# Sliding the moving operands of a two-layer MLP by 16 bytes per revolution of their ring

## The chip, the cores and the metric

The kernel runs on one core of one Trainium2 chip. The metric is device time in microseconds (us) of one execution; lower is better. The engines that matter are TensorE (PE in the rows; its weight loads have a row kind of their own, PEld), VectorE (DVE), ScalarE (ACT), GpSimd (POOL) and SyncE (SP), which here only issues DMAs.

## The reference, cut to what matters

```python
X = np.fft.rfft(x, axis=1)                       # x: 8 x 3008 x 256
y = np.fft.irfft(X * (filt_r + 1j * filt_i)[None], n=3008, axis=1)
x = y.reshape(24064, 256)
h = x @ w_in                                     # 256 -> 2048
P = a[0] + a[1] * h + a[2] * h**2 + a[3] * h**3
Q = 1 + abs(b[0]) * abs(h) + abs(b[1]) * h**2
out = (P / (Q + 1e-6)) @ w_out                   # 2048 -> 256
```

A long convolution by Fourier transforms along the sequence, then an MLP with a rational activation on 24064 tokens.

## The kernel before

The tokens are cut into 47 tiles of 512 (`T`), and the 2048 hidden features into 16 blocks of 128. One tile with one block is a *unit*: 752 units, the last of them split into two halves of 256 tokens, so 753. Both products of the MLP are done with a split of each float32 number into an upper and a lower part of type fp32r: upper times upper, upper times lower, lower times upper. One unit therefore has six matmuls for the first product (`product_in`, lines 631, 632 and 634: two of each, over the two halves of the 256 input features) and six for the second (`product_out`, lines 714, 715 and 716: two of each, over the two halves of the 256 outputs). In all twelve the weights are the stationary operand (128 x 128) and the tokens are the moving one (128 partitions x 512 columns of 4 bytes).

Where the moving operands lie:

- The split inputs are in one tile `xhl`, [128, 4, 1536] (`RX` = 1536 columns = three token tiles), whose first two rows are `xh` (upper parts of the two feature halves) and whose last two are `xl`. It is a ring: token s lies in column s % 1536. The ring goes round 15 times and two thirds in the 47 tiles. The convolution fills it chunk by chunk in `stage3`: float32 matmuls into PSUM (line 590), ScalarE writes the upper part (line 604), VectorE subtracts and writes the lower (line 606). Most chunks are 470 tokens long, and a chunk can start at any multiple of 47 tokens; a chunk that crosses the end of the ring is written in two parts.
- The results of the activation are in the tiles `hi` (five buffers) and `lo` (four), 128 x 512 of fp32r each. VectorE writes `hi` (`g_hi`, line 691) and `lo` (`g_lo`, line 705), GpSimd reads `hi` once (`pool_m`, line 696).

In the built program every tile named here starts at a multiple of 256 bytes within its partition, the weights `wi_sb` and `wo_sb` included (each 128 x 128 block of them is 512 bytes wide). So all twelve moving operands of every unit start at a multiple of 256 bytes, and so do their stationary operands. Two operands elsewhere do not: `e_sb`, the moving operand of line 590, starts 960 bytes into `small_sb`, so 192 bytes past a multiple of 256, and every second matmul of that line starts 188 bytes further, 124 bytes past one, which is not a multiple of 16 bytes. And the chunks that lines 604 and 606 write into the ring start at any multiple of 188 bytes.

The order of the instructions on PE, ACT, DVE and POOL is that in which the code issues them (a `manual_schedule`); a unit's second product is issued four units (`LAG`) after its first. Convolution steps are put between the units by a credit counter until the last batch is done. All DMAs are issued by SyncE.

Of the kernel before, what the change touches and what calls it, by code (L numbers as in the profile page):

```python
# [10 lines left out]
F32R = mybir.dt.float32r  # L11
# [26 lines left out]
RING = dict(a=4, w=3, q=5, hi=5, lo=4)  # L38
# [22 lines left out]
T = 512  # L61
RX = 1536
TT = 512


def shape_constants():
# [116 lines left out]
def conv_moe(ctx: ExitStack, tc: tile.TileContext, xp, filt, w_in, w_out, mats, small, sgn, outT):  # L183
    nc = tc.nc
    B = xp.shape[0]

    consts = ctx.enter_context(tc.tile_pool(name="consts", bufs=1))
    dram = ctx.enter_context(tc.tile_pool(name="dram", bufs=3, space=DRAM))
    conv = ctx.enter_context(tc.tile_pool(name="conv", bufs=2))
    mlp = ctx.enter_context(tc.tile_pool(name="mlp", bufs=1))  # L190
# [3 lines left out]
    sgn_sb = consts.tile([128, 32], F32, name="sgn_sb")  # L194
    wi_sb = consts.tile([128, 4, 2, 2, TT], F32R, name="wi_sb")
    wo_sb = consts.tile([128, 8, 2, TT], F32R, name="wo_sb")
    tin0 = consts.tile([128, K2, C], F32, tag="xhl", name="tin0")
# [53 lines left out]
    class Weights:  # L251
# [12 lines left out]
        def load(self):  # L264
# [5 lines left out]
            else:  # L270
                raw = conv.tile([128, TT, 2], U32, tag=tag, name=f"raw{i}", **({"bufs": bufs} if bufs else {}))
            self.l, self.h = raw[:, :, 0], raw[:, :, 1]
            nc.sync.dma_start(raw.rearrange("p c t -> p (c t)"), self.src)

        def room(self):
            i = self.i
            if i in FIRST:
                self.p, self.t = (
                    mlp.tile([128, TT], U32, tag=slots[2 * (FIRST.index(i) % 8) + n], name=f"{x}{i}")
                    for n, x in enumerate(("wp", "wt"))  # L280
                )
            else:
                pt = conv.tile([128, 2, TT], U32, tag="f2", name=f"wp{i}", bufs=FB)
                self.p, self.t = pt[:, 0], pt[:, 1]
# [54 lines left out]
    def w_in_part(k, f, cc):  # L339
        return wi_sb[:, f // 4, cc, k, f % 4 * 128 : f % 4 * 128 + 128]  # L340
# [19 lines left out]
    class Banks:  # L360
# [5 lines left out]
        def tile(self, name):  # L366
            k = min(self.free, key=self.free.get)
            del self.free[k]
            return k, ps.tile([128, TT], F32, tag=f"h{k}", name=name)

# [200 lines left out]
    def stage3(k):  # L571

        b, r, n = chunks[k]
        tiles, five = n * 2 // 5 if n % 5 == 0 else n // 2, n % 5 == 0
        tl = conv.tile([128, 4, C], F32, tag="tl", name=f"tl{k}")
        scr = scr2[b].rearrange("k (e r) c -> (k e) r c", e=2)
        for h in range(2):
            nc.sync.dma_start(tl[h * RH : h * RH + RH, :tiles], scr[:, r + h * tiles : r + h * tiles + tiles])
        if five:
            src = scr[:, r + 2 * tiles : r + n].rearrange("(k e) s c -> k e (s c)", e=2)  # L580
            nc.sync.dma_start(tl[2 * RH : 2 * RH + K2].rearrange("p (e s) c -> p e (s c)", e=2), src)
        if five:
            steps = [(2 * RH + K2, 2 * e + s, 5 * s + 2 * e, 1 - e, 4 - e) for s in range(2) for e in range(2)]
        else:
            steps = [(2 * RH, u, 2 * u, 1, 3) for u in range(tiles)]
        for cc in range(2):
            yield 1.1
            bank, pt = banks.tile(f"x_{k}_{cc}")
            for m, (rows, u, o, e0, e1) in enumerate(steps):
                nc.tensor.matmul(  # L590
                    pt[:, o * N2 : (o + e1 - e0) * N2],
                    tl[:rows, u, cc * 128 : cc * 128 + 128],
                    e_sb[:rows, e0 * N2 : e1 * N2],
                    start=m == 0,
                    stop=m == len(steps) - 1,
                    skip_group_check=True,
                )
            yield

            t0, t1 = spans[k]  # L600
            cut = min(t1, (t0 // RX + 1) * RX)
            parts = [(slice(a % RX, a % RX + z - a), pt[:, a - t0 : z - t0]) for a, z in ((t0, cut), (cut, t1)) if a < z]
            for o, p in parts:
                nc.scalar.activation(xh[:, cc, o], p, AF.Copy)
            for o, p in parts:
                v.tensor_tensor(out=xl[:, cc, o], in0=p, in1=xh[:, cc, o].bitcast(F32), op=ALU.subtract)
            banks.done(bank, 0.5)

    xh = xl = None
    pos = {}  # L610

    class Unit:

# [4 lines left out]
            self.p0 = P0 if squares else A0  # L618

        def tile(self, tag, dt=F32):  # L620
            full = mlp.tile([128, TT], dt, tag=f"{tag}{self.i % RING[tag]}", name=f"{tag}_u{self.i}")
            return full[:, self.cols]

        def product_in(self):
            self.bank, o = banks.tile(f"h_u{self.i}")
            o = self.H = o[:, self.cols]
            first = self.t * T % RX
            ts = slice(first + self.cols.start, first + self.cols.stop)
            f = self.f
            for cc in range(2):  # L630
                nc.tensor.matmul(o, w_in_part(0, f, cc), xh[:, cc, ts], start=cc == 0, stop=False)  # L631
                nc.tensor.matmul(o, w_in_part(0, f, cc), xl[:, cc, ts], start=False, stop=False)  # L632
            for cc in range(2):
                nc.tensor.matmul(o, w_in_part(1, f, cc), xh[:, cc, ts], start=False, stop=cc == 1)  # L634
# [103 lines left out]
    whole, parts = slice(0, T), [slice(c, c + T // LAST) for c in range(0, T, T // LAST)]  # L738
# [14 lines left out]
    def head():  # L753

        plan = Plan(8 - T * 2 // TT, dict(xin=XB, oe=2, tl=2, ev=2, f1=FB, f2=FB, raw=1))
        s = Stage2(0)
        first, sums, pts, yts, zts, pair = {}, {}, {}, {}, {}, []

        def x_load(t):
            n, tag = width(t), ("xin", "xin", "xin", "xin", "oe", "oe", "tl")[t]  # L760
            if tag == "tl":
                tile = conv.tile([128, 4, C], F32, tag=tag, name=f"xin0_{t}")[:, :2]
            else:
                tile = conv.tile([128, 2, n], F32, tag=tag, name=f"xin0_{t}", **({"bufs": XB} if tag == "xin" else {}))
            first[t] = stage1_load(0, t, tile)
# [4 lines left out]
        def load_pair():  # L770
            tile = mlp.tile([128, TT], F32, tag=slots[20], name="pair")
            nc.sync.dma_start(tile, mats.rearrange("p m c -> p (m c)"))
            pair.extend(tile[:, k * 128 : k * 128 + 128] for k in range(4))
# [110 lines left out]
        for k, i in enumerate(FIRST):  # L884
# [16 lines left out]
            add(f"{n}upper", w.upper, "ACT", 0.53, [f"{n}whole"], due=late - 1, filler=True)  # L901
            add(f"{n}lower", w.lower, "POOL", 1.25, [f"{n}upper"], due=late - 2, filler=True)
        xs = [stage3(k) for k in range(2)]

        def split():
            nonlocal xh, xl
            xhl = consts.tile([128, 4, RX], F32R, tag="xhl", name="xhl")
            xh, xl = xhl[:, :2], xhl[:, 2:]

        for k, x in enumerate(xs):  # L910
            step = lambda x=x: next(x, None)
            if k == 0:
                add("split", split, "ACT", 0.0, ["y11"], due=190)
            add(f"tl{k}", step, "SP", 0.5, ["zst5"], due=-4, moves=1.4 if k == 0 else 0.3, ring=("tl", f"xe{k}1"))
            for cc in range(2):
                add(f"xm{k}{cc}", step, "PE", 2.15 if k == 0 else 0.43, [f"tl{k}", "split"] + ([f"xe{k}0"] if cc else []), due=200 + k, bank=f"xe{k}{cc}")
                add(f"xe{k}{cc}", step, "ACT", 0.5 if k == 0 else 0.25, [f"xm{k}{cc}"], due=200 + k, then=[("DVE", 0.65 if k == 0 else 0.25)])
        plan.run()

    def pipeline(squares):  # L920
# [10 lines left out]
        for i in range(n + LAG + 2 * OG):  # L931
# [31 lines left out]
            if i < n and f in (XF, XF + 8) and not xgen and xk < len(chunks):  # L963
                c0, c1 = spans[xk]
                need = chunks[xk][0]
                if c1 <= t * T + RX and ((c0 if f > XF else c1) < T * (t + 2) or need < nxt):
                    if need >= nxt:
                        run(gen or conv_items(nxt))
                        gen, active = None, None
                        nxt += 1  # L970
                    xgen = stage3(xk)
                    xk += 1
                    next(xgen)
                    xi = i
# [131 lines left out]
```

## Time and profile before

| | |
|---|---|
| time, median of 2 runs | 2482.96 us (2482.76 to 2483.16) |
| span of the profiled execution | 2480.0 us; its own time is not given apart, the median is 2.96 us above the span |
| mean granted TensorE clock | 0.994; full in the windows from 200 to 2400 us |
| PE busy | 2431.0 us, 98% |
| ACT busy | 2348.5 us, 95% |
| DVE busy | 2277.8 us, 92% |
| POOL busy | 2089.9 us, 84% |

The first 100 us are the first batch's convolution and the preparation of the weights. From there to about 2000 us, MLP units and the convolution of later batches run side by side; after that only MLP units and the last chunks of the ring are left. PE's busy time is modelled (matmuls overlap in their pipeline), so how long a matmul holds the engine is read from the distance between two starts, not from its duration in a row.

### The profile page before, as it was taken

The numbers are of one execution on the slowest core, as the hardware profiler recorded it, in microseconds if no ns is written. First come the engines' busy times: TensorE is split into PE (matmuls) and PEld (weight loads), VectorE is DVE, ScalarE is ACT, GpSimd is POOL, SyncE is SP. The second block draws the span as 40 slices with busy tenths as digits, with TensorE's granted clock in tenths as the row PEclk, the third lists the DMA queues.
The fourth block names the chain that finished last, engine by engine and source line by source line (L and its number), as shares of the span: only waits on it lengthen the run. The fifth ranks groups of instructions, "written<-read, shape, count | busy, mean of one in ns | idle before, by whom it ended". The sixth has DMA issues, their size and how long they took to land.

```text
span 2480.0 us, 36386 instructions
## 1 busy us (share of the span) xinstructions
PE 2431.0 (98%) x10770; PEld 1941.0 (78%) x10770; DVE 2277.8 (92%) x3568; ACT 2348.5 (95%) x4178; POOL 2089.9 (84%) x2240
## 2 busy tenths in 40 slices
PE   7699999999999999999999999999999999999999
PEld 4577777878778787787787877878778788888887
DVE  7789988999899998999889998999889999999998
ACT  6799999999999999999999999999999999999998
POOL 7788887898879987899878997889879887888898
PEclk8899999999999999999999999999999999999999
DMA  7533332322323232332323322332222210100000
GB/s 260 151 111 108 94 106 84 102 85 72 108 90 93 85 87 73 110 90 83 95 79 102 92 80 80 95 103 90 86 79 85 68 37 17 34 26 17 21 9 19
DMA packets 102423, 205.15 MB, mean 83 GB/s; under 512 B 9455, under 2 KB 55855, under 8 KB 102215
## 3 DMA queue, kind: packets, MB, share of 16 engines
q1 hardware_dynamic: 102215, 202.74, 27.0%
q8 instruction: 87, 1.43, 0.2%
q14 instruction: 121, 0.99, 0.1%
HBM read 130.53 MB, written 72.17 MB: 82 GB/s over the span
## 4 chain that ended last, share of the span: by engine, by line
PE 76%; ACT 8%; POOL 6%; DVE 6%; issue 3%; DMA 1%; SPq 0%; DVEq 0%; POOLq 0%; ACTq 0%
PE o L715 11%; PE o L714 11%; PE o L716 11%; PE h_u L631 11%; PE h_u L632 11%; PE h_u L634 11%; PE s L444 3%; PE x L590 3%; POOL q_u L696 3%; PE y L497 2%; PE z L358 2%; ACT q_u L652 2%; ACT q_u L639 2%; POOL q_u L677 1%; ACT a_u L657 1%
## 5 line engine op out<-in xcount | busy, mean ns | idle before, releaser
L696 POOL TENSOR_TENSOR q_u<-q_u,hi_u 128x512 f32<-128x512 f32 x753 | 975.4, 1295 | 246.5 <-DVE hi_u L691 226.7
L714 PE MATMUL o<-hi_u,wo_sb 128*128 128x512 f32 x1506 | 661.4, 439 | 0.0
L691 DVE SCALAR_TENSOR_TENSOR hi_u<-h_u,scal,a_u 128x512 fp32r<-128x512 f32 x753 | 557.4, 740 | 52.4 <-ACT a_u L667 44.1
L631 PE MATMUL h_u<-xhl,wi_sb 128*128 128x512 f32 x1506 | 592.6, 394 | 6.1 <-DVE raw L325 4.0
L715 PE MATMUL o<-lo_u,wo_sb 128*128 128x512 f32 x1506 | 588.5, 391 | 7.9 <-DVE lo_u L705 7.7
L716 PE MATMUL o<-hi_u,wo_sb 128*128 128x512 f32 x1506 | 587.6, 390 | 0.0
L632 PE MATMUL h_u<-xhl,wi_sb 128*128 128x512 f32 x1506 | 587.3, 390 | 0.0
L699 DVE SCALAR_TENSOR_TENSOR h_u<-h_u,scal,q_u 128x512 f32<-128x512 f32 x753 | 563.7, 749 | 24.2 <-POOL q_u L696 22.9
L682 DVE SCALAR_TENSOR_TENSOR h_u<-w_u,scal,h_u 128x512 f32<-128x512 f32 x753 | 560.3, 744 | 5.2 <-ACT w_u L646 5.2
L657 ACT ACTIVATE a_u<-q_u,scal 128x512 f32<-128x512 f32 x753 | 549.3, 729 | 0.0
L652 ACT ACTIVATE q_u<-q_u,scal 128x512 f32<-128x512 f32 x753 | 547.2, 727 | 1.9
L677 POOL TENSOR_SCALAR q_u<-q_u,scal 128x512 f32<-128x512 f32 x753 | 525.5, 698 | 1.5 <-ACT a_u L657 1.4
L646 ACT ACTIVATE w_u<-h_u,scal 128x512 f32<-128x512 f32 x753 | 518.8, 689 | 0.0
L705 DVE TENSOR_TENSOR lo_u<-h_u,a_u 128x512 fp32r<-128x512 f32 x753 | 512.5, 681 | 0.1
L639 ACT ACTIVATE q_u<-h_u 128x512 f32<-128x512 f32 x753 | 453.6, 602 | 56.6 <-PE h_u L634 46.8
L634 PE MATMUL h_u<-xhl,wi_sb 128*128 128x512 f32 x1506 | 464.5, 390 | 0.0
L667 ACT ACTIVATE a_u<-a_u 128x512 f32<-128x512 f32 x688 | 438.4, 637 | 0.3
L715 PEld LDWEIGHTS o<-lo_u,wo_sb 128*128 128x128 f32 x1506 | 283.3, 188 | 97.7 <-issue 37.0
L714 PEld LDWEIGHTS o<-hi_u,wo_sb 128*128 128x128 f32 x1506 | 283.0, 188 | 88.8 <-issue 36.9
L631 PEld LDWEIGHTS h_u<-xhl,wi_sb 128*128 128x128 f32 x1506 | 283.3, 188 | 74.3 <-DVE lo_u L705 8.8
L632 PEld LDWEIGHTS h_u<-xhl,wi_sb 128*128 128x128 f32 x1506 | 283.4, 188 | 60.4 <-issue 1.3
L716 PEld LDWEIGHTS o<-hi_u,wo_sb 128*128 128x128 f32 x1506 | 282.6, 188 | 60.9
(94 smaller groups left out, 2221.8 us busy)
## 6 DMA issues: line engine op xcount, KB each, us to landing
f<-filt SPq DMA_DIRECT2D x168, 256.0 KB
xin<-xp SPq DMA_DIRECT2D x48, 512.0 KB
scr<-ev SPq DMA_DIRECT2D x48, 512.0 KB
outT<-oe SPq DMA_DIRECT2D x46, 512.0 KB
xin<-scr SPq DMA_DIRECT2D x42, 512.0 KB
scr<-xin SPq DMA_DIRECT2D x42, 480.0 KB
tl<-scr SPq DMA_DIRECT2D x96, 192.0 KB
tl<-scr SPq DMA_DIRECT2D x62, 96.0 KB
```

The lines of the kernel that those rows point to most:

```text
L631: nc.tensor.matmul(o, w_in_part(0, f, cc), xh[:, cc, ts], start=cc == 0, stop=False)
L632: nc.tensor.matmul(o, w_in_part(0, f, cc), xl[:, cc, ts], start=False, stop=False)
L634: nc.tensor.matmul(o, w_in_part(1, f, cc), xh[:, cc, ts], start=False, stop=cc == 1)
L652: nc.scalar.activation(self.q, self.q, AF.Square, bias=QC)
L657: nc.scalar.activation(self.a, self.q, AF.Abs_reciprocal_sqrt, bias=QK)
L682: v.scalar_tensor_tensor(out=H, in0=w, scalar=PK, in1=H, op0=ALU.add, op1=ALU.mult)
L691: nc.vector.scalar_tensor_tensor(out=self.hi, in0=self.H, scalar=self.p0, in1=self.a, op0=ALU.add, op1=ALU.mult)
L696: nc.gpsimd.tensor_tensor(out=self.q, in0=self.q, in1=self.hi.bitcast(F32), op=ALU.mult)
L699: nc.vector.scalar_tensor_tensor(out=self.H, in0=self.H, scalar=self.p0, in1=self.q, op0=ALU.add, op1=ALU.subtract)
L714: nc.tensor.matmul(o, w_out_part(0, f, dd), self.hi, start=f == 0 and self.cols.start == 0, stop=False)
L715: nc.tensor.matmul(o, w_out_part(0, f, dd), self.lo, start=False, stop=False)
L716: nc.tensor.matmul(o, w_out_part(1, f, dd), self.hi, start=False, stop=f == 15 and self.cols.stop == T)
```

## The change

Two constants are added, `MOVE` = 60 and `STEP` = 4 columns of 4 bytes. A function `at` gives the column of a token: s % 1536 as before, plus 60, minus 4 for each revolution. So in the first revolution every token tile lies 240 bytes further than before, in the second 224, and so on down to 0 in the sixteenth. The rows of `xhl` become 64 columns (256 bytes) longer to hold that. Tiles `hi` and `lo` become 64 columns longer too, and the part used of them is shifted by the same number of columns as the token tile that the unit works on. So all twelve matmuls of a unit read their moving operand that far past a multiple of 256 bytes; what writes these operands, and what else reads them (lines 604, 606, 691, 705 and 696), uses the shifted addresses. Because the longer tiles need space, the scratch that is set aside for DMAs whose descriptors software writes is halved to 8192 bytes per partition, and all tiles behind it move by multiples of 256 bytes.

On every engine the built program holds the same instructions as before in the same order (17447 rows on PE in both), with the same semaphores waited for and raised; only addresses differ.

```diff
+MOVE, STEP = 60, 4
...
-            parts = [(slice(a % RX, a % RX + z - a), pt[:, a - t0 : z - t0]) for a, z in ((t0, cut), (cut, t1)) if a < z]
+            parts = [(slice(at(a), at(a) + z - a), pt[:, a - t0 : z - t0]) for a, z in ((t0, cut), (cut, t1)) if a < z]
...
+    def at(s):
+        return s % RX + MOVE - STEP * (s // RX)
...
         def tile(self, tag, dt=F32):
-            full = mlp.tile([128, TT], dt, tag=f"{tag}{self.i % RING[tag]}", name=f"{tag}_u{self.i}")
-            return full[:, self.cols]
+            wide = 64 if tag in ("hi", "lo") else 0
+            first = at(self.t * T) - self.t * T % RX if wide else 0
+            full = mlp.tile([128, TT + wide], dt, tag=f"{tag}{self.i % RING[tag]}", name=f"{tag}_u{self.i}")
+            return full[:, first + self.cols.start : first + self.cols.stop]
 
         def product_in(self):
...
-            first = self.t * T % RX
+            first = at(self.t * T)
...
-            xhl = consts.tile([128, 4, RX], F32R, tag="xhl", name="xhl")
+            xhl = consts.tile([128, 4, RX + 64], F32R, tag="xhl", name="xhl")
...
-    nc = bacc.Bacc("TRN2", target_bir_lowering=False, num_devices=1)
+    nc = bacc.Bacc("TRN2", target_bir_lowering=False, num_devices=1, dynamic_dma_scratch_size=8192)
```

## Rows read from the trace of the kernel before

**Rows 1.** The page's head, its busy times (part 1) and its chain (part 4).
```profile
span 2480.0 us, 36386 instructions
PE 2431.0 (98%) x10770; PEld 1941.0 (78%) x10770; DVE 2277.8 (92%) x3568; ACT 2348.5 (95%) x4178; POOL 2089.9 (84%) x2240
...
PE 76%; ACT 8%; POOL 6%; DVE 6%; issue 3%; DMA 1%; SPq 0%; DVEq 0%; POOLq 0%; ACTq 0%
PE o L715 11%; PE o L714 11%; PE o L716 11%; PE h_u L631 11%; PE h_u L632 11%; PE h_u L634 11%; PE s L444 3%; PE x L590 3%; POOL q_u L696 3%; PE y L497 2%; PE z L358 2%; ACT q_u L652 2%; ACT q_u L639 2%; POOL q_u L677 1%; ACT a_u L657 1%
```
**Rows 2.** Windows by stage: stretch, length, busy us (instructions) by engine, clock, DMA.
```profile
core 0: us, PE busy (x) PEld busy (x) DVE busy (x) ACT busy (x) POOL busy (x), PEclk, DMA share, GB/s
...
200.00:1100.00 900.00, 894.25 (x3919) 713.28 (x3918) 832.78 (x1304) 870.13 (x1562) 765.46 (x824) 1.00 0.31 92
1100.00:2000.00 900.00, 897.66 (x3937) 716.92 (x3936) 834.49 (x1304) 863.88 (x1543) 771.17 (x839) 1.00 0.29 86
2000.00:2400.00 400.00, 399.90 (x1830) 332.71 (x1829) 381.65 (x600) 387.69 (x681) 332.91 (x341) 1.00 0.08 25
```
**Rows 3.** Waits: us in total, times, longest us.
```profile
POOL q_u L696 <- DVE hi_u L691: 226.7, 209, 3.8
...
PE x L590 <- DMA tl<-scr: 8.0, 1, 8.0
PE o L715 <- DVE lo_u L705: 7.7, 4, 3.7
```
**Rows 4.** Timeline of PE, 2207.9 to 2248 us: first and last rows of 175 steps.
```profile
start us, us, engine line op out<-in xcount [idle before <-releaser]
...
2208.04 0.39 PE L714 MATMUL o<-hi_u,wo_sb 128*128 128x512 f32 x1
...
2247.71 0.61 PE L634 MATMUL h_u<-xhl,wi_sb 128*128 128x512 f32 x2
```
**Rows 5.** Timeline of PE in the split last unit, 256 columns each.
```profile
2465.36 0.28 PE L632 MATMUL h_u<-xhl,wi_sb 128*128 128x256 f32 x1
2465.48 0.28 PE L631 MATMUL h_u<-xhl,wi_sb 128*128 128x256 f32 x1
2465.60 0.28 PE L632 MATMUL h_u<-xhl,wi_sb 128*128 128x256 f32 x1
2465.72 0.40 PE L634 MATMUL h_u<-xhl,wi_sb 128*128 128x256 f32 x2
2465.96 0.40 PE L714 MATMUL o<-hi_u,wo_sb 128*128 128x512 f32 x1
```
**Rows 6.** The costliest groups (part 5): the matmuls and the users of hi and lo.
```profile
L696 POOL TENSOR_TENSOR q_u<-q_u,hi_u 128x512 f32<-128x512 f32 x753 | 975.4, 1295 | 246.5 <-DVE hi_u L691 226.7
L714 PE MATMUL o<-hi_u,wo_sb 128*128 128x512 f32 x1506 | 661.4, 439 | 0.0
L691 DVE SCALAR_TENSOR_TENSOR hi_u<-h_u,scal,a_u 128x512 fp32r<-128x512 f32 x753 | 557.4, 740 | 52.4 <-ACT a_u L667 44.1
L705 DVE TENSOR_TENSOR lo_u<-h_u,a_u 128x512 fp32r<-128x512 f32 x753 | 512.5, 681 | 0.1
```
**Rows 7.** Timeline of PE around one chunk's line 590 (eight passes of 141 columns).
```profile
728.57 1.13 PE L590 MATMUL x<-small_sb,tl 120*128 120x141 f32 x8
729.44 0.49 PE L714 MATMUL o<-hi_u,wo_sb 128*128 128x512 f32 x1
729.77 0.40 PE L715 MATMUL o<-lo_u,wo_sb 128*128 128x512 f32 x1
```
**Rows 8.** Timeline of DVE: writes of 470 columns into the ring (line 606).
```profile
81.21 0.65 DVE L606 TENSOR_TENSOR xhl<-x,xhl 128x470 fp32r<-128x470 f32 x1 [0.79 <-ACT xhl L604]
92.06 0.65 DVE L606 TENSOR_TENSOR xhl<-x,xhl 128x470 fp32r<-128x470 f32 x1 [1.92 <-ACT xhl L604]
205.87 0.65 DVE L606 TENSOR_TENSOR xhl<-x,xhl 128x470 fp32r<-128x470 f32 x1 [0.29 <-ACT xhl L604]
260.15 0.65 DVE L606 TENSOR_TENSOR xhl<-x,xhl 128x470 fp32r<-128x470 f32 x1 [1.41 <-ACT xhl L604]
```
**Rows 9.** DMA queues (part 3): packets, MB, share of 16 engines' span.
```profile
q1 hardware_dynamic: 102215, 202.74, 27.0%
q8 instruction: 87, 1.43, 0.2%
q14 instruction: 121, 0.99, 0.1%
```

## The prediction

> **What bounds the kernel now.** I read the page's busy times and its chain first: PE is busy for 98% of the span and holds 76% of the chain, 11% for each of the six lines of the MLP's matmuls [rows 1]. Since a share over the whole span can hide stages, I then read the windows by stage: from 200 to 2000 us PE is busy 1791.9 of 1800 us, from 2000 to 2400 us 399.9 of 400, both at the full clock [rows 2]. The next engine is ACT with 870.1, 863.9 and 387.7 us in the three windows; DVE and POOL have more room. The list of waits says the same: the longest waits of PE on another party are 8.0 and 7.7 us in total [rows 3]. So what a matmul costs PE goes into the time one for one, and what other engines lose is first covered by their slack.
>
> How long one matmul holds PE is the distance between starts. In a stretch without convolution, 175 steps lie between 2208.04 and 2247.71 us [rows 4]: 39.67 / 175 = 226.7 ns. In the split last unit, five steps of 256 columns lie between 2465.36 and 2465.96 us [rows 5]: 120 ns. The difference, 106.7 ns for 256 columns, is 2.4 columns per ns, one per cycle at the upper of the two clock levels. So 512 columns take 213.3 ns, and **13.3 ns of each matmul do not depend on its length**. An effect of where the operand starts can sit only in this part, or beside it.
>
> **The change, part by part.** No instruction is added, removed or moved, and no wait is added: every engine's list is the same. What is left is the price of addresses.
>
> *Matmuls.* Tiles 0 to 44 (revolutions 0 to 14) get an operand that starts off a multiple of 256 bytes; tiles 45 and 46 (revolution 15, offset 0) keep what they had. 45 tiles x 16 blocks x 12 = 8640 matmuls. The trace has no fp32r matmul that starts off a multiple of 256, so I bound the price from both sides. Nearest rows: line 590 reads a moving operand that starts alternately 192 and 124 bytes past a multiple of 256. From its first start to that of L715 in the next unit are 729.77 - 728.57 = 1.20 us [rows 7]; one 512-column matmul (0.227) lies in it, so 0.973 us go to eight passes: 121.7 ns each. These float32 passes take two cycles per column: 141 columns / 1.2 per ns = 117.5 ns. At most 4.2 ns of a pass are left for everything else, the start included, although half of the passes start at an address that isn't even a multiple of 16 bytes. That speaks for a price of zero; its limit is that a pass reads at half the rate of an fp32r matmul, so that a late first piece could hide. Above, the largest price that rows give is a second helping of the fixed part, +13.3 ns; below, its loss, -13.3 ns. I take 0, since the row with shifted starts lies nearest to it.
>
> The Trainium skill, "SBUF — State Buffer", section "Door 1: The DMA port swizzle" (its note on cachelines), says that SBUF has lines of 16 bytes and that a crossing to a new line pays. By it the sum is 0 as well, because a shift by multiples of 16 leaves 2048 bytes on 128 lines, and the larger pieces of the second and third case below do not exist; no run here shows the size of a line.
>
> *Writers and readers of the shifted tiles.* DVE writes the ring at many starts: the 470 columns at 81.21 us start at the ring's column 0, those at 92.06, 205.87 and 260.15 us are 208, 216 and 48 bytes past a multiple of 256 (tokens 564, 1974 and 2444, modulo 1536, times 4), and each takes 0.65 us [rows 8]. Line 606 also reads the upper part there. So lines 606, 691 and 705 cost nothing more; line 604 writes the same ranges, and ACT is given nothing for it. POOL's read of `hi` is the one access that no row shows at a shifted start. If it read in pieces of 64 bytes and needed one more of 33, 1295 / 32 = 40 ns for 753 instructions would be 30 us (an estimate from [rows 6]), covered by the 246.5 us that POOL stands idle ahead of that line. Without that cover it would delay DVE's line 699, not PE, which takes the unit's result four units later. Price 0.
>
> *Scratch.* Every DMA is on a hardware queue or fetches instructions [rows 9], so a smaller area for software descriptors touches nothing. Price 0.
>
> **Sum:** 8640 x 0 + 0 + 0 = 0 us on a span of 2480.0; the median of the runs is 2.96 us above the span, and I keep that distance: 2483 us.
>
> **The rivals.** A difference of 2%, 49.7 us, is about what a measurement of this kernel can tell from no change. On 8640 matmuls that is 5.75 ns each.
>
> 1. *No effect* (the forecast): 2483 us, within some 9 us for a nanosecond per matmul either way.
>
> 2. *One more small piece per operand.* If the operand comes in pieces of 32 or 64 bytes, a start inside one makes 2048 bytes take one piece more. At 2.4 columns or 9.6 bytes per ns that is 3.3 or 6.7 ns. For 32 bytes every second revolution is off (24 tiles, 4608 matmuls): +15 us, 2498 us. For 64 bytes three of four are off (36 tiles, 6912 matmuls): +46 us, 2529 us. For it speaks that PE has no slack; against it [rows 7]. Both stay just within 2%.
>
> 3. *The fixed part is a piece of 128 bytes* (13.3 ns x 9.6 = 128 bytes; slower by over 2%). That the two numbers meet is what speaks for it: if each matmul pays one piece of that size to start, a start inside a piece pays another. Only offsets 128 and 0 (5 tiles) stay free; 42 tiles or 8064 matmuls x 13.3 = +107 us: 2590 us. From a piece of about 70 bytes upwards this case is slower by more than 2%. Against it: line 590's 4.2 ns, and that the fixed part can as well be the change of weights that each matmul has.
>
> 4. *The fixed part is a collision of two reads* (faster). Moving and stationary operands both start at multiples of 256 bytes now, and a matmul starts with the next weight load beside it. If the 13.3 ns come from that and any shift ends them, PE gains 8640 x 13.3 = 115 us. ACT then binds: it is busy 1734 of 1800 us and 387.7 of 400, which leaves 66 + 12 = 78 us: 2405 us. For it: line 590, with shifted starts, has 4 ns where fp32r has 13. Against it: the float32 passes may have these 4 ns because they read at half the rate.
>
> The Trainium skill, "TensorE: Matmul & The Clock Gate", section "Wait — 56ns, not 53.3ns?", gives about 2.5 ns per matmul over its columns at the upper clock. The trace disagrees, with 13.3 [rows 4, 5]; if the shift brought the page's figure, PE would gain 8640 x 10.8 = 93 us, and the same bound by ACT would leave 2405 us. What no page and no row says is that the start address is the reason, so this adds nothing to the chance of the fourth case.
>
> **How the numbers follow.** No effect 0.62, small piece 0.18, large piece 0.12, collision 0.08. The likeliest gives the time, 2483 us, with 2474 to 2492 as its own range. The range for 8 in 10 takes in the small pieces up to 64 bytes: 2472 to 2531 us; the two cases outside it hold 0.20 together. Slower by over 2% is the third case, 0.12; faster by over 2% the fourth, 0.08; within 2% the rest, 0.80.
>
> **What would show it.** The change is its own ruler: a revolution is about a sixteenth of the span, some 150 us, so distances between starts in dense stretches at 150, 300, ... 2400 us show sixteen offsets in one trace. Right: 226.7 ns in all of them. Second case: 230 or 233 ns in revolutions off the piece, 226.7 in the others, a saw-tooth in steps of two or four revolutions. Third: 240 ns except in revolutions 7 and 15. Fourth: 213 to 216 ns in revolutions 0 to 14 and 226.7 in the last, with ACT's idle time gone. DVE's 740 and 681 ns and POOL's 1295 ns [rows 6] should stand as they are; a POOL time that changes with the offset would refute the price for line 696, one that lets PE wait for `lo` would refute its cover. I am wrong if an offset changes the 226.7 ns by more than a nanosecond.

## The result, and the profile after

The changed kernel takes 2517.7 us (median of 2 runs, 2517.13 to 2518.27) against 2482.96 us: ratio 1.0145, interval 1.0116 to 1.0175. It is 34.7 us slower, clear of noise and within the 2% and the range that were forecast, but it is not the "no effect" that the forecast held for likeliest, whose own range ended at 2492 us.

Head, busy times and chain of the page of the changed kernel, which answer to [rows 1]:

```profile
span 2516.5 us, 36386 instructions
PE 2471.3 (98%) x10770; PEld 1943.6 (77%) x10770; DVE 2280.6 (91%) x3568; ACT 2357.0 (94%) x4178; POOL 2093.0 (83%) x2240
...
PE 83%; POOL 5%; ACT 4%; DVE 4%; issue 2%; DMA 1%; SPq 0%; POOLq 0%; DVEq 0%; ACTq 0%
```

The span grows by 36.5 us and PE's busy time by 40.3; the other engines are busy for as long as before, within 9 us. PE's share of the chain (the work that ended last, followed back) rises from 76% to 83%. The windows by stage (columns as in [rows 2]) show the same from another side: PE is as full as it was, and gets less done in the same time.

```profile
200.00:1100.00 900.00, 896.63 (x3852) 703.37 (x3851) 820.66 (x1282) 859.37 (x1534) 754.94 (x812) 1.00 0.30 90
1100.00:2000.00 900.00, 898.66 (x3889) 707.84 (x3887) 822.81 (x1286) 855.33 (x1527) 759.45 (x823) 1.00 0.29 86
2000.00:2400.00 400.00, 399.96 (x1791) 325.63 (x1790) 373.85 (x587) 381.14 (x668) 327.69 (x338) 1.00 0.08 26
```

In the last window 1791 matmul records stand where there were 1830, at the full clock. So each matmul holds PE longer. The costliest groups, which answer to [rows 6], say that it is PE alone:

```profile
L702 POOL TENSOR_TENSOR q_u<-q_u,hi_u 128x512 f32<-128x512 f32 x753 | 975.3, 1295 | 261.8 <-DVE hi_u L697 241.5
L697 DVE SCALAR_TENSOR_TENSOR hi_u<-h_u,scal,a_u 128x512 fp32r<-128x512 f32 x753 | 561.4, 746 | 60.4 <-ACT a_u L673 55.0
L688 DVE SCALAR_TENSOR_TENSOR h_u<-w_u,scal,h_u 128x512 f32<-128x512 f32 x753 | 563.5, 748 | 5.2 <-ACT w_u L652 5.2
```

POOL's read of the shifted `hi` takes 1295 ns as before. DVE's write of `hi` takes 746 ns for 740, but line 688, which touches no shifted tile, has moved from 744 to 748 as well. In the page of the kernel before it is line 682:

```profile
L682 DVE SCALAR_TENSOR_TENSOR h_u<-w_u,scal,h_u 128x512 f32<-128x512 f32 x753 | 560.3, 744 | 5.2 <-ACT w_u L646 5.2
```

POOL's idle time ahead of line 702 grew from 246.5 to 261.8 us; the row puts it down to DVE's `hi`, which itself waits longer for ACT (55.0 us for 44.1).

The distances between starts tell how much longer, and where. Each pair of lines below is the first and the last row of a stretch of PE's timeline without convolution (start us, us, engine, line and so on). They lie in revolutions 0, 3, 7, 11, 12 (two stretches), 14 and 15, where the moving operands are 240, 192, 128, 64, 48, 16 and 0 bytes past a multiple of 256:

```profile
97.69 0.40 PE L722 MATMUL o<-hi_u,wo_sb 128*128 128x512 f32 x1
...
111.41 0.39 PE L720 MATMUL o<-hi_u,wo_sb 128*128 128x512 f32 x1
...
626.20 0.40 PE L720 MATMUL o<-hi_u,wo_sb 128*128 128x512 f32 x1
...
638.34 0.62 PE L640 MATMUL h_u<-xhl,wi_sb 128*128 128x512 f32 x2
...
1289.58 0.40 PE L721 MATMUL o<-lo_u,wo_sb 128*128 128x512 f32 x1
...
1302.83 0.62 PE L640 MATMUL h_u<-xhl,wi_sb 128*128 128x512 f32 x2
...
1864.57 0.39 PE L721 MATMUL o<-lo_u,wo_sb 128*128 128x512 f32 x1
...
1877.62 0.62 PE L640 MATMUL h_u<-xhl,wi_sb 128*128 128x512 f32 x2
...
2066.24 0.40 PE L720 MATMUL o<-hi_u,wo_sb 128*128 128x512 f32 x1
...
2093.76 0.63 PE L640 MATMUL h_u<-xhl,wi_sb 128*128 128x512 f32 x2
...
2099.15 0.39 PE L721 MATMUL o<-lo_u,wo_sb 128*128 128x512 f32 x1
...
2133.42 0.39 PE L637 MATMUL h_u<-xhl,wi_sb 128*128 128x512 f32 x1
...
2332.76 0.39 PE L721 MATMUL o<-lo_u,wo_sb 128*128 128x512 f32 x1
...
2373.76 0.63 PE L640 MATMUL h_u<-xhl,wi_sb 128*128 128x512 f32 x2
...
2429.85 0.39 PE L637 MATMUL h_u<-xhl,wi_sb 128*128 128x512 f32 x1
...
2461.81 0.39 PE L638 MATMUL h_u<-xhl,wi_sb 128*128 128x512 f32 x1
```

They hold 58, 52, 57, 57, 118, 149, 177 and 141 steps:

| offset, bytes | distance, us / steps | one step, ns |
|---|---|---|
| 240 | 13.72 / 58 | 236.6 |
| 192 | 12.14 / 52 | 233.5 |
| 128 | 13.25 / 57 | 232.5 |
| 64 | 13.05 / 57 | 228.9 |
| 48 | 27.52 / 118 | 233.2 |
| 48 | 34.27 / 149 | 230.0 |
| 16 | 41.00 / 177 | 231.6 |
| 0 | 31.96 / 141 | 226.7 |

Over all steps between MLP matmuls of a revolution, those next to the convolution's stretches included, the means of revolutions 0 to 14 lie between 230.7 and 235.0 ns. **Every offset but 0 is slow, and a rounder offset is not free.** The loss does not hang on the offset alone: the two stretches at 48 have the same starts modulo 256 and differ by 3 ns. So the figure of one stretch is good to a few ns as a price of its offset. What chooses between the two was not tested.

The sum, from all distances between starts in both traces (an MLP matmul followed by another, less than 250 ns later): 8345 steps of 227.22 ns before, 8343 of 232.15 after, so 1896.1 and 1936.8 us, +40.7. All distances with a matmul of the convolution or the head (the work before the first unit) on either side come to 4.5 us less, the few long ones (321 and 323) to 0.2 us less. That is +36.0 of the span's +36.5 us.

### The profile page after: what moved, and what is told of

It is laid out like the page before. It is cut to its first block, busy times and chain, and to the rows that moved or that the text cites. A ratio compares the mean times of both kernels' runs of the same rounds, so it can differ in the third digit from the quotient of the medians.

```text
span 2516.5 us, 36386 instructions
## 1 busy us (share of the span) xinstructions
PE 2471.3 (98%) x10770; PEld 1943.6 (77%) x10770; DVE 2280.6 (91%) x3568; ACT 2357.0 (94%) x4178; POOL 2093.0 (83%) x2240
## 4 chain that ended last, share of the span: by engine, by line
PE 83%; POOL 5%; ACT 4%; DVE 4%; issue 2%; DMA 1%; SPq 0%; POOLq 0%; DVEq 0%; ACTq 0%
PE o L721 12%; PE o L722 12%; PE o L720 12%; PE h_u L637 12%; PE h_u L640 12%; PE h_u L638 12%; PE s L445 3%; PE x L591 3%; PE y L498 3%; PE z L359 2%; POOL q_u L702 2%; POOL q_u L683 1%; ACT q_u L658 1%; ACT q_u L645 1%; DVE h_u L705 1%
## 5 line engine op out<-in xcount | busy, mean ns | idle before, releaser
L702 POOL TENSOR_TENSOR q_u<-q_u,hi_u 128x512 f32<-128x512 f32 x753 | 975.3, 1295 | 261.8 <-DVE hi_u L697 241.5
L637 PE MATMUL h_u<-xhl,wi_sb 128*128 128x512 f32 x1506 | 601.1, 399 | 5.5 <-DVE raw L326 4.2
L638 PE MATMUL h_u<-xhl,wi_sb 128*128 128x512 f32 x1506 | 594.6, 395 | 0.0
L640 PE MATMUL h_u<-xhl,wi_sb 128*128 128x512 f32 x1506 | 472.4, 395 | 0.0
L720 PEld LDWEIGHTS o<-hi_u,wo_sb 128*128 128x128 f32 x1506 | 283.4, 188 | 93.4 <-issue 36.9
L637 PEld LDWEIGHTS h_u<-xhl,wi_sb 128*128 128x128 f32 x1506 | 283.9, 189 | 79.7 <-DVE lo_u L711 6.6
L638 PEld LDWEIGHTS h_u<-xhl,wi_sb 128*128 128x128 f32 x1506 | 283.8, 188 | 67.4 <-issue 1.7
L640 PEld LDWEIGHTS h_u<-xhl,wi_sb 128*128 128x128 f32 x1506 | 283.6, 188 | 67.0
```

The lines of the kernel that those rows point to most:

```text
L702: nc.gpsimd.tensor_tensor(out=self.q, in0=self.q, in1=self.hi.bitcast(F32), op=ALU.mult)
L720: nc.tensor.matmul(o, w_out_part(0, f, dd), self.hi, start=f == 0 and self.cols.start == 0, stop=False)
```

## The experiments

All kernels start from the changed one. In each the step (the distance between two starts) is measured in one and the same stretch of the program, from line 721's matmul (line 722 or 723 where the edit adds lines) behind a chunk of the ring to the next chunk: 177 steps to the last row shown. In the kernel before that stretch has 226.7 ns. Three theories stood at the beginning: A, the start of the moving operand alone costs; R, what costs is its distance from the start of the weights, modulo 256; L, the new layout as such costs.

**m0: the layout without the shift.**

```diff
-MOVE, STEP = 60, 4
+MOVE, STEP = 0, 0
```

> The changed kernel with MOVE = 0 and STEP = 0: the longer tiles, the longer rows of the ring and the smaller scratch stay, every operand starts at a multiple of 256 bytes again. Theory A (the start address of the moving operand alone costs: one that is off a multiple of 256 bytes pays about 5.5 ns) and theory R (what costs is the distance of the moving operand's start from that of the weights, modulo 256 bytes): 226.7 ns per step, ratio 1.000 within 0.002. Theory L (the new layout as such costs: rows of 6400 bytes, other places of the tiles): the time of the changed kernel, ratio 1.014.

Ratio 0.9994 (0.9985 to 1.0004). PE's timeline, first and last row of the stretch:

```profile
2210.84 0.40 PE L721 MATMUL o<-lo_u,wo_sb 128*128 128x512 f32 x1
...
2250.97 0.62 PE L640 MATMUL h_u<-xhl,wi_sb 128*128 128x512 f32 x2
```

40.13 / 177 = 226.7 ns. Theory L is out: longer tiles, longer rows and the smaller scratch cost nothing.

**m128, w128, mw128: who has to be aligned with whom.** m128 shifts the moving operands by 128 bytes in every revolution (`MOVE, STEP = 32, 0`). w128 leaves them at 0 and shifts the weights; mw128 does both.

```diff
+    wi_w = consts.tile([128, 16 * TT + 64], F32R, name="wi_sb")
+    wo_w = consts.tile([128, 16 * TT + 64], F32R, name="wo_sb")
+    wi_sb = wi_w[:, 32 : 32 + 16 * TT].rearrange("p (a b c t) -> p a b c t", a=4, b=2, c=2)
+    wo_sb = wo_w[:, 32 : 32 + 16 * TT].rearrange("p (a c t) -> p a c t", a=8, c=2)
```

> MOVE = 32 columns, STEP = 0: every moving operand of the MLP lies 128 bytes past a multiple of 256 in every revolution. Theories A and R: every revolution behaves as revolution 7 of the changed kernel did (mean step 232.5 ns, +5.3 ns), 9036 x 5.3 = +48 us, ratio 1.019, band 1.014 to 1.023. A piece of 64 or 128 bytes (the second and third cases of the prediction): no cost at this offset, ratio 1.000.

> MOVE = 0, but the weight tiles wi_sb and wo_sb start 128 bytes later, so that the stationary operands lie 128 bytes past a multiple of 256 and the moving ones at 0. Theory A: 226.7 ns, ratio 1.000. Theory R: the same distance as in m128, about 232 ns, ratio about 1.019. A third outcome, both starts costing by themselves, would look like R here and is told apart by mw128.

> MOVE = 32 columns and the weight tiles 128 bytes later too: both operands are 128 bytes past a multiple of 256, their distance is 0. Theory A: as m128, 232 ns, ratio about 1.019. Theory R: 226.7 ns, ratio 1.000. If both starts cost by themselves: 235 ns or more, ratio above 1.025.

m128: ratio 1.0143 (1.0126 to 1.0160). w128: 1.0149 (1.0132 to 1.0166). mw128: 0.9994 (0.9985 to 1.0004). The stretch in PE's timeline, m128 first:

```profile
2239.25 0.39 PE L721 MATMUL o<-lo_u,wo_sb 128*128 128x512 f32 x1
...
2280.37 0.39 PE L640 MATMUL h_u<-xhl,wi_sb 128*128 128x512 f32 x1
```

w128:

```profile
2237.63 0.39 PE L723 MATMUL o<-lo_u,wo_sb 128*128 128x512 f32 x1
...
2278.92 0.63 PE L642 MATMUL h_u<-xhl,wi_sb 128*128 128x512 f32 x2
```

mw128:

```profile
2208.41 0.39 PE L723 MATMUL o<-lo_u,wo_sb 128*128 128x512 f32 x1
...
2248.53 0.62 PE L642 MATMUL h_u<-xhl,wi_sb 128*128 128x512 f32 x2
```

41.12 / 177 = 232.3 ns, 41.29 / 177 = 233.3, 40.12 / 177 = 226.7. The weights may be the ones that are shifted, with every moving operand at a multiple of 256, and the loss is the same; shift both and it is gone. Theory A falls. At this offset theory R holds: what counts is how the moving operand and the weights lie to each other. That PE's reads of the two disturb each other is the nearest explanation; the runs show the time, not the reads. (The nanosecond between 232.3 and 233.3 is no difference between the kernels: each has both values, in different stretches. m128's ratio is below the expected 1.019 because 8344 steps grew by 5.0 ns on the mean, 41.6 us in all, where 9036 times 5.3 was expected, and because the distances at the convolution's matmuls gave 3.7 us back.)

**wo128: which weights.** Only `wo_sb`, the weights of the second product, starts 128 bytes later; the moving operands are at 0.

```diff
+    wo_w = consts.tile([128, 16 * TT + 64], F32R, name="wo_sb")
+    wo_sb = wo_w[:, 32 : 32 + 16 * TT].rearrange("p (a c t) -> p a c t", a=8, c=2)
```

> MOVE = 0 and only the weights of the second product, wo_sb, start 128 bytes later. Theory N (while a matmul streams, what it collides with is the load of the next matmul's weights, which the trace shows starting 3 ns after the matmul's start): slow steps, about 232 ns, are those whose next matmul is one of the second product, the step from the last matmul of the first product into the second among them, and the last matmul of a second product that is followed by a first product stays at 226.7 ns. Theory O (the matmul's own weights count): the opposite at these two places, the six steps of the second product slow and no other. Both: half of the steps slow, 4518 x 5.3 = +24 us, less some us that waits take up, ratio 1.007 to 1.009.

Ratio 1.0093 (1.0076 to 1.0110). The stretch:

```profile
2225.77 0.40 PE L722 MATMUL o<-lo_u,wo_sb 128*128 128x512 f32 x1
...
2266.62 0.62 PE L641 MATMUL h_u<-xhl,wi_sb 128*128 128x512 f32 x2
```

40.85 / 177 = 230.8 ns. Mean steps by their place in the unit, from the starts in units 620 to 749 (101 to 130 steps each): within the first product 226.8 to 227.7 ns, from its last matmul into the second 232.5, within the second 229.2 to 239.2, from the second into the next first product 232.7, and the step behind that 231.0. The first of the two changes is slow, against theory O; the second is slow too, against theory N. Neither holds alone.

**pair128: each product aligned in itself.** First product (`xhl`, `wi_sb`) at 128, second (`hi`, `lo`, `wo_sb`) at 0.

```diff
-MOVE, STEP = 60, 4
+MOVE, STEP = 32, 0
...
-            first = at(self.t * T) - self.t * T % RX if wide else 0
+            first = 0
...
+    wi_w = consts.tile([128, 16 * TT + 64], F32R, name="wi_sb")
+    wi_sb = wi_w[:, 32 : 32 + 16 * TT].rearrange("p (a b c t) -> p a b c t", a=4, b=2, c=2)
```

> The first product's operands, xhl and wi_sb, lie 128 bytes past a multiple of 256, the second product's, hi, lo and wo_sb, at 0: every matmul has distance 0 to its own weights. Theory O (own weights count): 226.7 ns everywhere, ratio 1.000. Theory N (the load of the next weights, beside the stream, counts): only the two steps at which the products change are slow, about 232 ns, 1506 x 5.3 = +8 us, ratio 1.003. If a step also needs one or two steps behind it to settle, as in wo128 (231 ns in the step behind the change back): +16 to +24 us, ratio 1.006 to 1.010.

Ratio 1.0043 (1.0026 to 1.0060), +10.5 us on medians. The stretch, and a matmul of the second product with the load that runs beside it:

```profile
2219.08 0.39 PE L722 MATMUL o<-lo_u,wo_sb 128*128 128x512 f32 x1
...
2259.51 0.62 PE L641 MATMUL h_u<-xhl,wi_sb 128*128 128x512 f32 x2
```

```profile
2220.00 0.40 PE L723 MATMUL o<-hi_u,wo_sb 128*128 128x512 f32 x1
2220.00 0.19 PEld L638 LDWEIGHTS h_u<-xhl,wi_sb 128*128 128x128 f32 x1
```

40.43 / 177 = 228.4 ns. By place, as above: first into second product 232.7 ns, the step behind 230.5; second into first 233.2, the step behind 230.5; all others 226.4 to 227.7. Theory O falls: every matmul has the distance 0 to its own weights, and the changes between the products are slow. There the moving operand streams beside the load of weights that lie 128 bytes otherwise; the trace shows the load of the next matmul's weights starting 2 to 4 ns after the start of the matmul ahead of it. N with one or two further steps to settle fits this kernel and wo128. So does a rule by which the own weights and the next ones both count, with one step to settle behind; these two kernels do not tell them apart. The settling is read off the steps; its cause wasn't tested.

**half0 and half128: what the 13.3 ns are.** The matmuls with a lower part as moving operand (four of twelve) load only 64 columns of weights; half0 with `MOVE` 0, half128 with 32.

```diff
-                nc.tensor.matmul(o, w_in_part(0, f, cc), xl[:, cc, ts], start=False, stop=False)
+                nc.tensor.matmul(o[:64], w_in_part(0, f, cc)[:, :64], xl[:, cc, ts], start=False, stop=False)
...
-                nc.tensor.matmul(o, w_out_part(0, f, dd), self.lo, start=False, stop=False)
+                nc.tensor.matmul(o[:64], w_out_part(0, f, dd)[:, :64], self.lo, start=False, stop=False)
```

> MOVE = 0; the matmuls of the lower parts (upper weights times xl, upper weights times lo: four of the twelve of a unit) take only the first 64 columns of their weights and write 64 partitions of the result, so a small correction is left out in half of the outputs. It asks what the 13.3 ns are by which a step exceeds its 512 columns. Theory S (the weight load beside the stream takes reading time from it, in proportion to what it loads): 220 ns for the steps whose next matmul has 64 columns (N) or whose own has (O), 226.7 ns for the others. Theory F (a fixed price for each change of weights): 226.7 ns everywhere.

> As half0, with MOVE = 32: every moving operand lies 128 bytes past a multiple of 256, the weights at 0 (the same small correction left out). Theory S: the loss by the distance shrinks with the load, so steps beside a load of 64 columns take 220 to 223 ns and the others about 232. Theory F: about 232 ns everywhere.

One time each: half0 2499.07 us, half128 2518.66 us, the kernel before 2482.01. half0's stretch:

```profile
2220.97 0.39 PE L721 MATMUL o<-lo_u,wo_sb 128*64 128x512 f32 x1
...
2261.66 0.62 PE L640 MATMUL h_u<-xhl,wi_sb 128*128 128x512 f32 x2
```

40.69 / 177 = 229.9 ns: a third of the loads is halved, and the steps get *longer*. The values jump between 224 and 236 at nearly every place, those beside a full load too. half128 has 41.23 / 177 = 232.9 ns, from its starts in the same way, about what m128 has. Both theories fall as they were put: the steps neither shrink in proportion to what is loaded nor stay as they were. One reading is that the 226.7 ns need loads and streams that follow each other in an unbroken pattern; no run tests it, and the edit also halves the partitions that the four matmuls write. What sets the 13.3 ns stays open.

**m4, mw4, w4: off a multiple of 16 bytes.** `MOVE` = 1 column for m4 and mw4; mw4 and w4 have both weight tiles 4 bytes later.

```diff
-MOVE, STEP = 60, 4
+MOVE, STEP = 1, 0
```

> MOVE = 1 column, STEP = 0: all moving operands lie 4 bytes past a multiple of 256, which no revolution of the changed kernel tried. If the distance counts in lines of 16 bytes, 512 columns now touch 129 of them: about one column's worth more, or as offset 16 (231.5 ns). If any distance other than 0 breaks the pattern: 231 to 235 ns, +35 to +45 us. If distances under 16 bytes are free: 226.7 ns, ratio 1.000.

> MOVE = 1 column and both weight tiles 4 bytes later too: moving and stationary operands all lie 4 bytes past a multiple of 256, at distance 0. Theory R alone (only the distance counts): 226.7 ns, ratio 1.000. If what m4 lost beyond offset 16 (236.7 against 231.5 ns) is the price of a 129th line of 16 bytes, whatever the distance: 230 to 232 ns, ratio 1.013 to 1.019. If the start as such is what counts: 236 to 237 ns as in m4, ratio about 1.029.

> MOVE = 0, both weight tiles 4 bytes later: the moving operands start on a multiple of 256, the stationary ones off a multiple of 16. If the loss beyond 232 ns that m4 and mw4 showed belongs to the moving operand (129 lines of 16 bytes for 128): a distance that isn't 0, 231 to 233 ns, ratio 1.014 to 1.017. If it belongs as much to the weight load (33 lines for 32): 235 to 238 ns, ratio 1.026 to 1.033.

m4: 2554.57 us, one run (+72.6). mw4: ratio 1.0325 (1.0308 to 1.0342). w4: 1.0144 (1.0127 to 1.0161). The stretch in m4, mw4 and w4, in this order, one fence each:

```profile
2269.74 0.40 PE L721 MATMUL o<-lo_u,wo_sb 128*128 128x512 f32 x1
...
2311.63 0.63 PE L640 MATMUL h_u<-xhl,wi_sb 128*128 128x512 f32 x2
```

```profile
2274.41 0.40 PE L723 MATMUL o<-lo_u,wo_sb 128*128 128x512 f32 x1
...
2316.50 0.64 PE L642 MATMUL h_u<-xhl,wi_sb 128*128 128x512 f32 x2
```

```profile
2238.35 0.39 PE L723 MATMUL o<-lo_u,wo_sb 128*128 128x512 f32 x1
...
2279.48 0.63 PE L642 MATMUL h_u<-xhl,wi_sb 128*128 128x512 f32 x2
```

41.89 / 177 = 236.7 ns, 42.09 / 177 = 237.8, 41.13 / 177 = 232.4. A moving operand off a multiple of 16 loses 10 ns per step, and here a distance of 0 saves nothing: mw4 is no better than m4. Weights off a multiple of 16 under an aligned moving operand (w4) lose no more than weights at 128 (w128). So among these kernels the extra 5 ns, 236.7 against 231.6 ns at offset 16, come with the moving operand's own start. A rule of the Trainium skill would have that sign ("SBUF — State Buffer", note on cachelines in "Door 1: The DMA port swizzle": lines of 16 bytes, a crossing to a new one costs); the rule has no figure for it. But the changed kernel has 236.6 ns at offset 240 too, which is a multiple of 16. So these runs don't show that the line of 16 bytes is the reason.

**mw16: does the distance alone count?** `MOVE, STEP = 4, 0` and both weight tiles 16 bytes later.

> MOVE = 4 columns and both weight tiles 16 bytes later: moving and stationary operands lie 16 bytes past a multiple of 256, at distance 0, where revolution 14 of the changed kernel (offset 16, weights at 0) had 231.5 ns. If, among starts on a multiple of 16 bytes, only the distance counts: 226.7 ns, ratio 1.000. If mw128 was free only because 128 is a multiple of some larger unit: 229 ns or more, ratio 1.007 or more.

Ratio 1.0100 (1.0084 to 1.0117).

```profile
2230.28 0.39 PE L723 MATMUL o<-lo_u,wo_sb 128*128 128x512 f32 x1
...
2271.18 0.63 PE L642 MATMUL h_u<-xhl,wi_sb 128*128 128x512 f32 x2
```

40.90 / 177 = 231.1 ns at distance 0, where the changed kernel had 231.6 at distance 16. Theory R as it was put falls. What stands: with moving operand and weights both at 0 or both at 128 a step takes 226.7 ns; with one of them at 0 and the other at 128, 232 to 233; with both at 16, 231. A rule that fits is that both have to start on some unit larger than 16 and no larger than 128 bytes, *and* that their distance counts. These few positions don't exclude another rule, and whether the unit is 32, 64 or 128 bytes wasn't tried.

No run beat the kernel before: its operands, all at multiples of 256 bytes, are the best of those tried, together with m0 and mw128.

## Why the prediction was right or wrong, point by point

- **What bounds the kernel: right.** PE had nothing to absorb a longer matmul. The MLP's steps grew by 40.7 us and the span by 36.5; the distances at the convolution's matmuls gave 4.5 back (why was not tested).
- **Price of a matmul's start, taken as 0: wrong.** It is 2 to 10 ns in dense stretches and 4.9 on the mean of all steps, so by the prediction's own sign (more than a nanosecond at any offset) its mechanism is refuted. The step that failed is the choice of the nearest row. Line 590's passes [rows 7] did show shifted starts at no more than 4.2 ns over their columns, but at half the reading rate, the limit named there, and that row says nothing of an fp32r matmul. Why the float32 passes are spared no run shows. Nor is the price one of the start alone, as the sum had it: with the weights shifted alike (mw128) it is 0 again. The bound of 13.3 ns on either side held for the mean of every run; the largest is mw4's, 237.8 - 226.7 = 11.1 ns.
- **The ruler: right, and it decided.** Offset 0 in revolution 15 stayed at 226.7 ns, all others were slow, in one trace. For the price of a single offset it is a rough ruler, as the two stretches at 48 show.
- **Second case, a small piece: right in time, wrong in mechanism.** Its 64-byte price gave 2529 us, and 2517.7 lies near it. But offsets 192, 128 and 64 should have been free, and had 233.5, 232.5 and 228.9 ns. Had only the time been measured, this case would have passed for the cause.
- **Third case, a piece of 128 bytes: wrong.** No revolution has 240 ns, and offset 128 is not free.
- **Fourth case, a collision of the two reads: the right two reads, the wrong sign.** How moving operand and weights lie to each other does count (m128, w128, mw128), but where both lie at 0 or both at 128 is the good position and not the bad one.
- **Writers, POOL and scratch at 0: right.** POOL's 1295 ns did not change with multiples of 16 bytes. DVE's 740 and 681 ns are 746 and 686 in the changed kernel, but 741 and 681 in m128 and 749 and 689 in half0, which shifts nothing: the shift is not what moves them. m0 shows that the smaller scratch costs nothing.
- **The range held by luck:** it reached up to 2531 us only because it took in the pieces up to 64 bytes, a mechanism that the runs refuted.

## What to carry to other kernels

Where PE is the bound and every fp32r matmul brings its own weights, let moving operands and weights both start at multiples of 256 bytes: of the other positions tried for both products, only that with all at 128 cost nothing; the rest cost 1 to 3% of the kernel. Before a row of another type is taken as the nearest price, ask whether it reads at the same rate. A sweep of a parameter over the length of one run, read from the distances between starts, shows in one trace where a loss lies; what it costs at one value, and why, still took kernels with that value throughout.

## What the runs showed of the hardware that was not expected

- The position of the *weights* costs as much as that of the moving operand: 233.3 ns (w128) and 232.3 (m128) for 226.7. The Trainium skill, "SBUF — State Buffer", section "Who interferes with whom", gives PE two independent read ports, one for each. If that is to mean that neither read can lengthen the other, the steps of these runs don't agree: m128 and mw128 differ in the position of the weights alone, w128 and mw128 in that of the moving operand alone, and mw128 has 226.7 ns.
- The same starts can settle on different steps, stretch by stretch: 233.2 and 230.0 ns at offset 48 in one trace.
- Fewer columns of weights to load, and fewer partitions to write, made the steps longer: 229.9 ns in half0 for 226.7 (one run).
- POOL became faster when one operand was off a multiple of 16 bytes. Its multiplication of `q` with `hi`, in the page of m4:

```profile
L702 POOL TENSOR_TENSOR q_u<-q_u,hi_u 128x512 f32<-128x512 f32 x753 | 825.2, 1096 | 339.7 <-DVE hi_u L697 320.6
```

1096 ns for 1295, and mw4 has the same with 1094. Here it brought no time: POOL's idle time ahead of that line grew from 246.5 to 339.7 us. Why it happens wasn't tried.
